# Clustered attention with a gated feed-forward: other places in the queue for the second batch's loads and rows

## The chip, the cores and the metric

The kernel runs on one core of one Trainium2 chip. The metric is the device time of one execution in microseconds (us). An engine takes its instructions in the order in which the program holds them. PE is the matmul engine (PEld its weight loads), DVE, ACT and POOL are the three elementwise engines, and SP issues nearly all transfers.

## The reference

Four batches of eight heads, 768 tokens, head width 64. Queries and keys are assigned to one of 16 centroids by the largest cosine; a query sees only keys of its own cluster. The result, 3072 tokens of 512 features, goes through a gated feed-forward.

```python
q_assign = np.argmax(np.einsum('bhsd,hcd->bhsc', q_n, c_n), axis=-1)
k_assign = np.argmax(np.einsum('bhsd,hcd->bhsc', k_n, c_n), axis=-1)
mask = q_assign[:, :, :, None] == k_assign[:, :, None, :]
scores = np.where(mask, scale * np.matmul(q, k.transpose(0, 1, 3, 2)), -1e9)
attn = softmax(scores)                      # over the keys
x = np.matmul(attn, v)                      # (tokens, 512) after regrouping the heads
out = (sigmoid(x @ w_gate) * (x @ w_val)) @ w_out
```

## The kernel before

The work goes by batch (0 to 3), and in a batch by pairs of heads (0 to 3; "first pair" is pair 0, and "second batch" is batch 1). The clock of the program is the **step**: one score matmul of 128 keys by 384 queries (L1071), its exponential on ACT (L1076) and, a few steps later, three matmuls with the values (L1094). There are 96 steps to a batch, 384 in all; a pair takes 24 of them, its two heads 12 each. Between the steps PE gets pieces of the feed-forward of the batch before (gate L537, value L553, output L870 and L999).

Before a pair's steps begin, its heads are prepared (`pair_prep`, from L1629). For each head these stages follow each other:

1. its raw keys and queries are loaded with those of the other head of the pair (`load`, L213: `kraw`, `qraw`, `vraw`, 384 KB each, three buffers to each kind);
2. `sp`: DVE casts to half precision (L1636), POOL takes the rest that the cast left (L1637); the two stand side by side in `hl`;
3. `tn`, the **turn**: SP issues a transposing transfer of `hl` into the tile `T` (L417, in the trace `T<-hl`);
4. `lg`: twelve small matmuls on PE (L441) read `T` and give the products with the centroids;
5. `pk`: DVE picks the largest and writes one-hot codes into `oh`; both heads of a pair share it;
6. `ot`: SP turns the codes (L1654, `ohT<-oh`);
7. `hp0` and `hp1`, the **rows**: SP copies the turned codes into rows 64 to 80 of the two tiles `T` (L497, two small transfers for each head). With these rows in both operands the score matmul applies the mask itself. The head's first score needs them.

The other transfers of SP are the turns of the attention's result for the feed-forward (L1125, `xTb<-xp`) and the stores (L509).

The order on every engine is set by the table `SCHED`: `at(step, f)` queues a piece of work, `run_bg` plays all pieces that are due, sorted by their step, and each engine's instructions come out in that order. A key such as `b1p3tn0` is an offset to the first step of batch 1, pair 3; `b1lk2` is one to the load of the keys of pair 2 (`lq` queries, `lv` values), added to the pair's `ld`. In batch 1 the pairs begin at steps 96, 120, 144 and 168, and batch 2 begins at 192.

```python
def go(name, off, f):
    o = SCHED.get(f"b{b}p{p}{name}", SCHED.get(f"b2{name}", off) if b > 1 else off)
    ...
    at(use + o, g)
...
at(use + o + d_, lambda b=b, p=p, side=side: load(..., SP, side, b, p))
```

The sign `E` in a key, as in `r3pl1E`, names the engine of a piece of batch 0 (A for ACT, D for DVE): here one of the two copies (L1403 on ACT, L1405 on DVE) that set the masking rows of the second half of batch 0's last pair.

Of the kernel before, what the change touches and what calls it, by code (L numbers as in the profile page):

```python
# [57 lines left out]
    "b1p2pk0": -35.5, "b1p2sp10": -50, "b1p2sp11": -47, "b1p2tn1": -42, "b1p2lg1": -28.0,  # L58
    "b1p2pk1": -27.0, "b1p2ot": -24, "b1p2hp0": -18, "b1p2hp1": -17.5, "b1p2vc": -18.0,
    "b1p2vs": -11.0, "b1p2vu": -2.5, "b1p2vt": 3, "b1p2ld": -67.5, "b1p2l20": 0, "b1p2le0":  # L60
    2.0, "b1p2l21": 0, "b1p2le1": 2.0, "b1p3sp00": -60.5, "b1p3sp01": -57, "b1p3tn0": -54,
    "b1p3lg0": -38.0, "b1p3pk0": -36.5, "b1p3sp10": -55.0, "b1p3sp11": -43.0, "b1p3tn1":
    -40.0, "b1p3lg1": -28, "b1p3pk1": -27.0, "b1p3ot": -23.5, "b1p3hp0": -13.0, "b1p3hp1":
    -12.5, "b1p3vc": -7.5, "b1p3vs": -18.5, "b1p3vu": -14.5, "b1p3vt": 4, "b1p3ld": -69.5,
# [7 lines left out]
    "dm2": 10, "dm3": 11, "dm4": 3, "la0": 3, "la1": 2, "lgop": 0, "h3ev1E": "A", "h4lo1E":  # L72
    "D", "r2hiE": "P", "r1pl0E": "A", "h5hi1E": "P", "h2hi0E": "A", "g0lo0E": "D", "h6ev1E":
    "A", "h2hi1E": "P", "h1lo1E": "D", "g1ev1E": "A", "r2ev0E": "A", "r1hiE": "P", "h4hi1E":
    "P", "r2pl1E": "A", "h3lo1E": "D", "r3pl1E": "A", "xm33": 1, "xm30": 1, "gL": 1, "rL3": 1,
    "rL2": 1, "rL1": 0, "rL0": 0, "gD": 0, "rD0": 0, "rD1": 0, "rD2": 0, "rD3": 1, "h4hi0E":
    "P", "xs00": -4, "xs10": 0, "xs01": -6, "xs11": 5.5, "xs02": 1, "xs12": 3.0, "xs03": -0.5,
    "xs13": 0, "sd": 1, "b2lk": -0.5, "b1lk0": 2.0, "b1lk1": -9, "b1lk2": -5, "b1lk3": -9.5,
    "b2lq": 0, "b1lq0": 2.5, "b1lq1": -0.5, "b1lq2": -4.9, "b1lq3": -9.4, "b2lv": 1.0, "b1lv0":
    -1, "b1lv1": 0.5, "b1lv2": 32.5, "b1lv3": 34, "ns02": 490, "ns03": 490, "ns20": 500,  # L80
    "ns21": 491, "ns22": 481, "ns23": 410, "ns30": 443, "ns31": 443, "ns32": 443, "ns33": 423,
    "h6hi1E": "P", "h1ev1E": "A", "g1hi0E": "A", "h3hi1E": "P", "g1lo0E": "D", "h1lo0E": "D",
    "r3pl0E": "A", "hM3": 0, "hM7": 1, "h1hi0E": "P", "g1hi1E": "P", "h3ev0E": "A", "g0pl0E":
# [9 lines left out]
    1, "tx": 1, "b2p3lk": 8.5, "b2p3lq": 9, "b2p3lv": 10, "b3p3lk": 8.5, "b3p3lq": 9,  # L93
    "b3p3lv": 10,
    "b3p0vs": -30, "b3p0vu": -28, "b3p0vt": -9, "b3p1lg0": -32, "b3p1pk0": -32, "fwg": [327, 327, 331, 331.5, 332, 341, 341, 344],
    "fwv": [354, 356, 357, 359, 364, 366, 370, 371], "b3p2pk1": -28.5, "b1p0sp00": -30, "b1p0sp01": -29, "b1p0sp10": -28, "b1p0sp11": -27, "b1p0tn0": -25.5, "b1p0tn1": -23.5, "b1p0lg0": -17, "b1p0pk0": -16, "b1p0lg1": -15.5, "b1p0pk1": -15.5, "b1p0ot": -14.5, "b1p0hp0": -8.5, "b1p0hp1": -8, "b2p0lk": 11, "b2p0lq": 11.5, "b2p0lv": 36, "b2p1lg1": -27, "b2p1pk1": -25.5, "nW20": 2.2, "END": 0,
}


# [1676 lines left out]
```

## Time and profile before

| | |
|---|---|
| median of 3 runs | 318.92 us (318.62 to 319.18) |
| the profiled execution | 319.96 us, of which 318.2 us span from first to last instruction |
| granted clock of PE | 1.000 |
| PE busy | 309.1 us (97%) |
| ACT, DVE, POOL busy | 241.7, 238.3, 122.0 us (76%, 75%, 38%) |
| SP's own DMA queue (q1) | 55.7% of 16 DMA engines' span, 40.75 MB |
| score matmuls | 384, 325 ns each by the modelled end |

The timeline gives for each group of instructions its start, its time, the engine, the line and the operands; a bracket at the end tells the idle time before it and what ended that. A PE row's end is modelled: the next matmul begins before it. A row of the transfers' view gives a kind of transfer, the number in the window, the size, and the time from issue to landing. SP rows show how long SP was busy with issuing.

### The profile page before, as it was taken

How to read it: one execution, taken by the hardware profiler on the slowest of the kernel's cores; microseconds unless marked ns; L12 is line 12 of the kernel's file. 1: busy time of each engine (PE TensorE's matmuls, PEld its weight loads, DVE VectorE, ACT ScalarE, POOL GpSimd, SP SyncE). 2: the span in 40 equal slices, each digit the busy share in tenths (PEclk: the TensorE clock that was granted, in tenths of full speed). 3: DMA queues.
4: the chain of work that ended last, by engine and by line, in shares of the span. 5: the costliest groups of instructions: out<-in, count | busy, mean ns of one | idle time of the engine just before them, and what ended most of it. 6: DMA issues, size and time to landing. Idle time of an engine off the chain costs nothing.

```text
span 318.2 us, 9151 instructions
## 1 busy us (share of the span) xinstructions
PE 309.1 (97%) x3444; PEld 217.0 (68%) x3444; DVE 238.3 (75%) x622; ACT 241.7 (76%) x550; POOL 122.0 (38%) x158
## 2 busy tenths in 40 slices
PE   7899999899999989999999999999999999999995
PEld 5688766555666655666777678766677678656684
DVE  6899658686887666686778688777888776678982
ACT  6788988667988877877866877788877887588621
POOL 5888447243434364423334233424212111026600
PEclk9999999999999999999999999999999999999999
DMA  7999999919699989889566467962803110300014
GB/s 212 369 262 165 269 175 170 226 34 207 185 210 248 186 196 179 230 152 198 111 186 149 135 136 104 256 175 49 111 5 82 48 27 12 146 1 1 2 35 165
DMA packets 82060, 46.24 MB, mean 145 GB/s; under 512 B 60896, under 2 KB 79584, under 8 KB 82016
## 3 DMA queue, kind: packets, MB, share of 16 engines
q1 hardware_dynamic: 77904, 40.75, 55.7%
q0 software_dynamic: 3680, 4.72, 8.9%
q8 instruction: 27, 0.44, 0.6%
q10 hardware_dynamic: 432, 0.20, 0.2%
q14 instruction: 17, 0.14, 0.2%
HBM read 28.34 MB, written 6.29 MB: 109 GB/s over the span
## 4 chain that ended last, share of the span: by engine, by line
PE 83%; DMA 9%; DVE 4%; SPq 1%; POOL 1%; issue 1%; ACT 1%; DVEq 0%
PE sc L1071 16%; PE g L537 13%; PE v L553 13%; PE av L1094 9%; PE o L999 9%; DMA T<-hl 7%; PE o L870 4%; PE lg L441 2%; PE o L704 2%; PE o_end L807 2%; PE av L704 2%; DMA kraw<-in_k_dram 2%; PE y L704 2%; PE v L633 2%; PE av L807 1%; PE o L807 1%
## 5 line engine op out<-in xcount | busy, mean ns | idle before, releaser
L1076 ACT ACTIVATE es<-sc 128x384 f16<-128x384 f32 x384 | 174.0, 492 | 42.6 <-PE sc L1071 31.3
L1071 PE MATMUL sc<-T 128*128 128x384 f16 x384 | 117.2, 325 | 0.6 <-DVE T L1405 0.2
L1094 PEld LDWEIGHTS <-es 128*128 128x128 f16 x1152 | 81.5, 98 | 35.1 <-ACT es L1076 0.2
L1094 PE MATMUL av<-va,es 128*128 128x65 f16 x1152 | 97.5, 194 | 0.0
L558 DVE SCALAR_TENSOR_TENSOR hT<-th,v 128x384 f16<-128x384 f32 x72 | 39.8, 553 | 33.3 <-PE av L1094 26.5
L377 POOL TENSOR_TENSOR xp<-t,rec 128x384 f16<-128x384 f32 (+1 forms) x30 | 21.7, 725 | 100.3 <-DVE rec L374 51.5
L553 PE MATMUL v<-xTb,wv 128*128 128x384 f16 x288 | 58.5, 326 | 0.3 <-ACT es L1076 0.2
L537 PE MATMUL g<-xTb,wg 128*128 128x384 f16 x288 | 58.5, 326 | 0.1
L543 ACT ACTIVATE th<-g 128x384 f32<-128x384 f32 x72 | 35.4, 492 | 8.4 <-PE g L537 6.1
L553 PEld LDWEIGHTS <-wv 128*128 128x128 f16 x288 | 28.0, 97 | 14.5 <-issue 0.9
L537 PEld LDWEIGHTS <-wg 128*128 128x128 f16 x288 | 28.0, 97 | 14.4 <-issue 0.3
L1071 PEld LDWEIGHTS <-T 128*128 128x128 f16 x384 | 37.0, 96 | 1.0 <-DVE T L1401 0.5
L1637 POOL TENSOR_TENSOR hl<-kraw,hl 128x384 f16<-128x384 f32 x24 | 22.2, 924 | 31.8 <-DVE hl L1636 17.5
L1637 POOL TENSOR_TENSOR hl<-qraw,hl 128x384 f16<-128x384 f32 x24 | 23.0, 958 | 12.4 <-DVE hl L1636 12.4
L372 DVE TENSOR_TENSOR t<-av,sv 128x390 f32<-128x390 f32 (+1 forms) x30 | 14.4, 480 | 7.5 <-PE av L1094 5.5
L870 PE MATMUL o<-wo,hT 128*128 128x512 f16 x72 | 19.9, 379 | 0.0
L946 DVE TENSOR_TENSOR ob<-o,ob 128x256 f32<-128x256 f32 (+1 forms) x28 | 15.0, 549 | 4.7 <-PE o L999 3.2
L713 POOL TENSOR_TENSOR hT<-T 128x384 f16<-128x384 f32 x12 | 11.8, 1004 | 16.2 <-DVE T L662 15.6
L456 DVE TENSOR_REDUCE lgs<-lg 128x192 f32<-128x384 f32 x24 | 13.2, 552 | 4.9 <-PE lg L441 4.9
L999 PE MATMUL o<-wo,hT 128*128 128x256 f16 x108 | 16.8, 272 | 0.0
L999 PEld LDWEIGHTS <-sum 128*128 128x128 f16 x144 | 14.0, 97 | 3.3
L324 POOL CAST va<-vraw 128x768 f16<-128x768 f32 x15 | 13.1, 875 | 2.3 <-DMA vraw<-in_v_dram 2.3
(207 smaller groups left out, 457.3 us busy)
## 6 DMA issues: line engine op xcount, KB each, us to landing
vraw<-in_v_dram SPq DMA_DIRECT2D x15, 384.0 KB, 5.9
kraw<-in_k_dram SPq DMA_DIRECT2D x14, 384.0 KB, 4.1
qraw<-in_q_dram SPq DMA_DIRECT2D x12, 384.0 KB, 4.5
out_dram<-ob SPq DMA_DIRECT2D x17, 256.0 KB, 2.3
wg<-in_moe_w_gate_dram POOLq DMA_DIRECT2D x2, 768.0 KB, 9.4
wv<-in_moe_w_val_dram POOLq DMA_DIRECT2D x2, 768.0 KB, 10.3
wo<-in_moe_w_out_dram POOLq DMA_DIRECT2D x2, 768.0 KB, 10.8
T<-ohT SPq DMA_DIRECT2D x48, 24.0 KB, 1.9
```

The lines of the kernel that those rows point to most:

```text
L377: (eng or POOL).tensor_tensor(x, t[:, 0:nq, 0:64], bcast(rec[:, 0:nq], 64), ALU.mult)
L537: PE.matmul(out=g[:, 0:n], lhsT=wg[fc // WQ][:, dc, fc % WQ, :], rhs=xT[:, dc, t0 : t0 + n], start=(dc == 0), stop=(dc == NDC - 1),)
L543: ACT.activation(th[:, 0:n], g[:, 0:n], AF.Tanh)
L553: PE.matmul(out=w[:, 0:n], lhsT=wv[fc // WQ][:, dc, fc % WQ, :], rhs=xT[:, dc, t0 : t0 + n], start=(dc == 0), stop=(dc == NDC - 1),)
L558: DVE.scalar_tensor_tensor(HB[b, blk][:, fc, 0:n], st[0][:, 0:n], 1.0, w[:, 0:n], ALU.add, ALU.mult)
L704: PE.matmul(out=o, lhsT=l, rhs=r, start=start and d == 0, stop=stop and d == 1, skip_group_check=True,)
L870: PE.matmul(out=o, lhsT=HB[b, blk][:, fc, bass.ts(t, 128)], rhs=wo[fc // WON][:, fc % WON, :], start=(fc == 0), stop=(fc == NFC - 1),)
L999: PE.matmul(out=st[z][:, e], lhsT=a[:, c, :], rhs=rhs[:, c, :], start=start and c + e == 0, stop=c == HF - 1, skip_group_check=True,)
L1071: PE.matmul(out=sc.rearrange("p (c t) -> p c t", t=128), lhsT=s["k"], rhs=s["q"], start=True, stop=True,)
L1076: ACT.activation(es, sc, AF.Exp, scale=SCALE)
L1094: PE.matmul(out=av[:, a0 + s["c0"] + i, :], lhsT=s["es"][:, bass.ts(i, 128)], rhs=VA[b, p][:, e, s["j"], :], start=(first and i == 0 and a ...
L1637: POOL.tensor_tensor(hl[:, :, 64:128], r, hl[:, :, 0:64], ALU.subtract)
```

## The change

Only numbers of `SCHED` change. In steps: the first pair's rows of batch 1 go from 87.5 and 88 to 86.5 and 87; the third pair's keys and queries from 71.5 to 78, its values from 109 to 90.5; the fourth pair's keys and queries from 89 to 90, its values from 132.5 to 94.5; its first head's casts from 107.5 and 111 to 106 and 108.5 and its first turn from 114 to 112. Of batch 2, the first pair's keys and queries go from 120.5 to 114 and its values from 145.5 to 109. One small copy of batch 0 goes from ACT to DVE.

```diff
-    "b1p3sp00": -60.5, "b1p3sp01": -57, "b1p3tn0": -54,
+    "b1p3sp00": -62, "b1p3sp01": -59.5, "b1p3tn0": -56,
...
-    "r3pl1E": "A"
+    "r3pl1E": "D"
...
-    "b1lk2": -5, "b1lk3": -9.5, "b1lq2": -4.9, "b1lq3": -9.4, "b1lv2": 32.5, "b1lv3": 34
+    "b1lk2": 1.5, "b1lk3": -8.5, "b1lq2": 1.6, "b1lq3": -8.4, "b1lv2": 14, "b1lv3": -4
...
-    "b1p0hp0": -8.5, "b1p0hp1": -8, "b2p0lk": 11, "b2p0lq": 11.5, "b2p0lv": 36
+    "b1p0hp0": -9.5, "b1p0hp1": -9, "b2p0lk": 4.5, "b2p0lq": 5, "b2p0lv": -0.5
```

What that makes of the order is shown at three places of SP. First, where batch 1's first two pairs are turned. `T_1467` and the next `T` (1505 before, 1501 now) are the first pair's two heads, 1572 (now 1568) and 1651 the second pair's; the raw tiles 1485 and 1497 (now 1598 and 1604) are the third pair's keys and queries. Before:

```order
L417 DMA_TRANSPOSE T_1467<-hl_1397 128x12x128
L213 DMA kraw_1485<-in_k_dram 128x2x384
L213 DMA qraw_1497<-in_q_dram 128x2x384
L417 DMA_TRANSPOSE T_1505<-hl_1431 128x12x128
L1125 DMA_TRANSPOSE xTb_312<-xp_1339 128x3x128
L417 DMA_TRANSPOSE T_1572<-hl_1478 128x12x128
L417 DMA_TRANSPOSE T_1651<-hl_1592 128x12x128
```

And now:

```order
L417 DMA_TRANSPOSE T_1467<-hl_1397 128x12x128
L417 DMA_TRANSPOSE T_1501<-hl_1431 128x12x128
L1125 DMA_TRANSPOSE xTb_312<-xp_1339 128x3x128
L417 DMA_TRANSPOSE T_1568<-hl_1478 128x12x128
L213 DMA kraw_1598<-in_k_dram 128x2x384
L213 DMA qraw_1604<-in_q_dram 128x2x384
L417 DMA_TRANSPOSE T_1651<-hl_1588 128x12x128
```

The two loads stood ahead of the first pair's second turn; now they stand ahead of the second pair's second turn.

Second, from the fourth pair's first turn (`T_2161`, now 2141) to its second (2349, now 2353). `ohT_2246` (now 2254) are the third pair's codes, the four copies from it that pair's rows, and the raw tiles 2252 and 2263 (now 2167 and 2173) are the keys and queries of batch 2's first pair. Before:

```order
L417 DMA_TRANSPOSE T_2161<-hl_2057 128x12x128
L1654 DMA_TRANSPOSE ohT_2246<-oh2_136 128x6x128
L213 DMA kraw_2252<-in_k_dram 128x2x384
L1125 DMA_TRANSPOSE xTb_1907<-xp_1945 128x6x128
L213 DMA qraw_2263<-in_q_dram 128x2x384
L497 DMA T_1858<-ohT_2246 16x768 x2
L497 DMA T_1997<-ohT_2246 16x768 x2
L417 DMA_TRANSPOSE T_2349<-hl_2151 128x12x128
```

And now:

```order
L417 DMA_TRANSPOSE T_2141<-hl_2049 128x12x128
L213 DMA kraw_2167<-in_k_dram 128x2x384
L213 DMA qraw_2173<-in_q_dram 128x2x384
L1654 DMA_TRANSPOSE ohT_2254<-oh2_136 128x6x128
L1125 DMA_TRANSPOSE xTb_1911<-xp_1949 128x6x128
L497 DMA T_1860<-ohT_2254 16x768 x2
L497 DMA T_2001<-ohT_2254 16x768 x2
L417 DMA_TRANSPOSE T_2353<-hl_2157 128x12x128
```

Here two loads that stood behind the turn of the codes now stand ahead of it.

Third, directly behind that: the loads of batch 2's second pair (2543, 2545, 2547; now 2545, 2547, 2549) and the turns of batch 2's first pair (2559 and 2683, now 2561 and 2683). Before:

```order
L213 DMA vraw_2416<-in_v_dram 128x2x384
L213 DMA kraw_2543<-in_k_dram 128x2x384
L213 DMA qraw_2545<-in_q_dram 128x2x384
L213 DMA vraw_2547<-in_v_dram 128x2x384
L417 DMA_TRANSPOSE T_2559<-hl_2446 128x12x128
L1654 DMA_TRANSPOSE ohT_2581<-oh0_134 128x6x128
L213 DMA vraw_2602<-in_v_dram 128x2x384
L1125 DMA_TRANSPOSE xTb_1907<-xp_2277 128x6x128
L417 DMA_TRANSPOSE T_2683<-hl_2552 128x12x128
```

And now:

```order
L213 DMA kraw_2545<-in_k_dram 128x2x384
L213 DMA qraw_2547<-in_q_dram 128x2x384
L213 DMA vraw_2549<-in_v_dram 128x2x384
L417 DMA_TRANSPOSE T_2561<-hl_2448 128x12x128
L1654 DMA_TRANSPOSE ohT_2583<-oh0_134 128x6x128
L1125 DMA_TRANSPOSE xTb_1911<-xp_2281 128x6x128
L417 DMA_TRANSPOSE T_2683<-hl_2554 128x12x128
```

The two value loads (2416, of the fourth pair, and 2602, of batch 2's first pair) have left this stretch. The three value loads that stood at steps 109, 132.5 and 145.5 now stand one ahead of the third pair's first turn, one ahead of the turn of the second pair's codes, and one ahead of the fourth pair's first turn, where the third pair's values stood. From the loads of batch 2's third pair on, the order of SP is the same as before.

12 rows, old and new, of the table SCHED are left out of this document.

## Prediction

> **What bounds the kernel now.** I read the page first, then the busy times by stage, then the waits, and last the timeline of the two queues that meet there. The page's busy line and three stretches of the table by stage (length, then busy time of PE, PEld, DVE, ACT, POOL):
>
> ```profile
> PE 309.1 (97%) x3444; PEld 217.0 (68%) x3444; DVE 238.3 (75%) x622; ACT 241.7 (76%) x550; POOL 122.0 (38%) x158
> 50.00:63.00 13.00, 12.15 (x135) 7.94 (x133) 10.15 (x27) 9.79 (x23) 6.54 (x8) 1.00 1.05 199
> 100.00:115.00 15.00, 14.11 (x165) 9.33 (x164) 10.66 (x32) 12.26 (x30) 6.37 (x7) 1.00 1.04 196
> 130.00:200.00 70.00, 69.93 (x782) 50.20 (x780) 53.15 (x137) 53.04 (x119) 22.72 (x27) 1.00 0.71 160
> ```
>
> PE sets the time. From 130 us on it has no hole to speak of (69.93 of 70), so a microsecond gained or lost ahead of that reaches the end almost whole. Its holes are in the stretches that the change touches: 0.85 us in the first, 0.89 us in the second. The waits tell what they are for:
>
> ```profile
> PEld L441 <- DMA T<-hl: 2.6, 4, 1.0
> PE lg L441 <- DMA T<-hl: 1.9, 3, 0.9
> ```
>
> The logits (L441) stand in PE's queue and wait for a turn `T<-hl` to land; everything behind them waits too. PE's timeline gives the four places (start, modelled time, line, and in the bracket the idle time):
>
> ```profile
> 57.99 0.32 PE L1071 MATMUL sc<-T 128*128 128x384 f16 x1
> 58.16 0.81 PE L537 MATMUL g<-xTb,wg 128*128 128x384 f16 x4
> ...
> 58.89 0.33 PE L1071 MATMUL sc<-T 128*128 128x384 f16 x1
> 59.79 0.47 PE L441 MATMUL lg<-cm,T 128*128 128x32 f16 x12 [0.57 <-DMA T<-hl]
> ...
> 98.23 0.26 PE L1094 MATMUL av<-va,es 128*128 128x65 f16 x3
> 98.59 0.46 PE L441 MATMUL lg<-cm,T 128*128 128x32 f16 x12
> ...
> 111.99 0.26 PE L1094 MATMUL av<-va,es 128*128 128x65 f16 x3
> 113.14 0.47 PE L441 MATMUL lg<-cm,T 128*128 128x32 f16 x12 [0.89 <-DMA T<-hl]
> ...
> 120.85 0.26 PE L1094 MATMUL av<-va,es 128*128 128x65 f16 x3
> 121.52 0.47 PE L441 MATMUL lg<-cm,T 128*128 128x32 f16 x12 [0.41 <-DMA T<-hl]
> ```
>
> The first two rows show an undisturbed pair: the score lasts 0.32 but the next matmul starts 0.17 after it, so each hole is its bracket plus 0.17. That makes 0.74 us at 59.8 (first pair of batch 1, second head), 1.06 at 113.1 and 0.58 at 121.5 (batch 2: first pair's second head, second pair's first). At 98.6 (fourth pair's second head) the start is 0.36 behind the last one, 0.10 over its 0.26, so 0.27 with the overlap. Sum 2.65 us. One more hole follows the first as its echo: ACT is behind and PE waits for it.
>
> ```profile
> 62.74 0.48 ACT L1403 ACTIVATE T<-oh_ps 16x384 f16<-16x384 f16 x1
> 62.77 0.81 PE L553 MATMUL v<-xTb,wv 128*128 128x384 f16 x4 [0.19 <-ACT es L1076]
> ```
>
> By the same count this one hole is 0.36 us. The copy on ACT is the one that the change gives to DVE.
>
> **Place one: the turn at 59.8.** SP's queue, the three transfers of it (time from issue to landing, last column), and the POOL row that completes that turn's data:
>
> ```profile
> 51.73 0.91 POOL L1637 TENSOR_TENSOR hl<-qraw,hl 128x384 f16<-128x384 f32 x1 [0.30 <-DVE hl L1636]
> ...
> 52.74 0.58 SPq L213 DMA_DIRECT2D kraw<-in_k_dram  x1
> 53.36 0.47 SPq L213 DMA_DIRECT2D qraw<-in_q_dram  x1
> 53.94 1.94 SPq L417 DMA_TRANSPOSE T<-hl  x1
> ...
> kraw<-in_k_dram SPq DMA_DIRECT2D x1, 384.0 KB, 4.3
> qraw<-in_q_dram SPq DMA_DIRECT2D x1, 384.0 KB, 4.9
> T<-hl SPq DMA_TRANSPOSE x1, 5.8
> ```
>
> Landings: keys 52.74 + 4.3 = 57.0, queries 58.3, turn 59.7. They land in the order of issue, about 1.3 us apart for a load and 1.5 for the turn: the queue behaves as one line. The data was ready at 52.64, so with the loads gone the turn is issued at 52.74, 1.2 us sooner, and has 2 x 1.3 us less ahead of it. Even if only the sooner issue counts it lands at 59.7 - 1.2 = 58.5; PE asks at 58.89 + 0.17 = 59.06. So the hole goes on either reading: **+0.74 us**. Of the echo I take +0.4: 0.36 by its row, and the copy's 0.48 us leaves ACT; DVE takes at most 0.5 us more there (it is busy 10.15 of 13). The bounds are 0 and 0.8.
>
> A rule that speaks against this: the Trainium skill, page "DMA: Bandwidth & Descriptors", section "Queues, rings and completion order", says that completion is not in order of issue for one issuing engine, so a load ahead need not hold the turn back. The three landings here are in order, so the trace does not show it at this place; what it would give is the second rival.
>
> The loads now stand ahead of the second pair's second turn, which has room:
>
> ```profile
> 58.27 3.00 SPq L417 DMA_TRANSPOSE T<-hl  x2
> ...
> 67.44 0.46 PE L441 MATMUL lg<-cm,T 128*128 128x32 f16 x12
> ```
>
> It is asked for 6 us after SP has issued it; two loads cost 2.6. Price 0.
>
> **Place two: the third pair's first turn.** The first pair's rows go ahead of an `xTb` turn. I assume that SP has room for their 2.49 us there, so that the loads and the turn behind move up by as much. In exchange one value load joins them.
>
> ```profile
> 69.23 2.49 SPq L497 DMA_DIRECT2D T<-ohT  x4
> ...
> 72.97 2.13 SPq L417 DMA_TRANSPOSE T<-hl  x1
> ...
> T<-hl SPq DMA_TRANSPOSE x1, 6.1
> ...
> 79.95 0.20 PE L441 MATMUL lg<-cm,T 128*128 128x32 f16 x2
> ```
>
> Today it lands at 79.0 and PE asks at 79.95. Up by 2.49, back by 1.3 for the extra load: 77.9. PE, ahead by 0.74 + 0.4, asks at 78.8. Room 0.9; I take 0. Without the credit it lands at 80.3 and PE waits 1.5; but then PE comes as much later to place three and waits so much less there, so the sum hardly moves. Behind it the turn of the second pair's codes also gets a value load ahead (1.3 us against the 2.49).
>
> **Place three: the fourth pair's second turn, at 98.6.** This is where the change can pay for itself twice.
>
> ```profile
> 84.65 0.96 POOL L1637 TENSOR_TENSOR hl<-qraw,hl 128x384 f16<-128x384 f32 x1 [0.76 <-DVE hl L1636]
> ...
> 85.64 1.33 SPq L417 DMA_TRANSPOSE T<-hl  x1
> 87.19 2.02 SPq L1654 DMA_TRANSPOSE ohT<-oh  x1
> ...
> 92.78 2.45 SPq L497 DMA_DIRECT2D T<-ohT  x4
> 95.28 1.35 SPq L417 DMA_TRANSPOSE T<-hl  x1
> ```
>
> SP cannot issue the rows (92.78) before the turned codes have landed, and the second turn stands behind them. So the chain is: codes land (92.7), rows 2.5 us, turn 3.3 us from issue to landing (95.28 to just before 98.59). Whatever delays the codes delays PE 5.8 us later. Now two loads stand ahead of the codes: +2.6 us. Against that, the first turn no longer waits for POOL at 85.61 (its casts stand 1.5 and 2.5 steps sooner, at about 0.65 us a step), so the chain starts about 1.0 us sooner; and a pause in this stretch should cost it less. The transfers between 89.5 and 91.5 hold one instruction fetch:
>
> ```profile
> q8 instruction: 1, 0.02, 3.6%
> ```
>
> I take it to come with PE's progress (PE has 3444 matmuls and as many weight loads, far the most instructions), so about 1.1 us sooner; today turn and codes are in flight then and both stand still, afterwards the loads are in flight and can go on beside it. I take 1.2 us for that (bounds 0 and 1.5; an estimate from the first turn's landing, some 1.5 us later than place one's spacing). The codes then land at 92.7 + 2.6 - 1.0 - 1.2 = 93.1, the second turn at 98.9. PE, 0.74 + 0.4 + 0.27 ahead, would ask at 98.59 - 1.4 = 97.2 and waits 1.7 us. It passes this place at 98.9 against 98.59 today: all that was gained by then is gone, and 0.3 us more. The bounds for the landing: 97.2 (no wait) and 101.1 (2.6 in full, no credit).
>
> **Place four: batch 2's first turns.** Two value loads leave this stretch.
>
> ```profile
> 105.45 0.58 SPq L213 DMA_DIRECT2D vraw<-in_v_dram  x1
> ...
> 107.44 2.17 SPq L417 DMA_TRANSPOSE T<-hl  x1
> ...
> 114.56 3.90 SPq L417 DMA_TRANSPOSE T<-hl  x1
> ```
>
> The turn issued at 107.44 lands as PE starts at 113.14. Without the load at 105.45 it is issued at least 0.6 us sooner with one load (1.3) less ahead: 1.9 against a hole of 1.06, which goes: **+1.06**. What follows on SP (rows, three loads, the turn at 114.56) moves up by as much, so the loads ahead of that turn have drained more when it comes; its hole of 0.58 goes, **+0.58** (bounds 0 and 0.58, since its own data may hold it). Nothing comes in their place: from there on the order is the old one and PE has the room.
>
> **The sum.** 98.59 - 98.9 + 1.06 + 0.58 = 1.3 us; less 0.1 for small waits, **1.2 us** gained. In general the gain is 100.2 minus the landing at place three, at most 3.0 us. Against the profiled execution (318.2 us span, 319.96 with what lies around it) that makes 318.8; the median of the runs is 318.92, 0.3% below that execution, so I forecast 318.92 - 1.2 = **317.7 us**. About 0.2% (0.64 us) is what a measurement of this kernel can tell from no change.
>
> **The rivals.**
> 1. *The codes behind the loads become the bound (slower).* If the landing at place three comes after 100.2, it costs more than place four returns. The full 2.6 us without credit gives 101.1, so 0.9 us lost: 319.8. With slower loads (up to 0.4 us more) 320.2. For it: SP's strict order and the 5.8 us chain. Against it: the sooner casts. Chance 0.28.
> 2. *The loads hold nothing back, or gain and loss cancel.* If turns are not in line behind loads, place four keeps 1.06 + 0.58, the turn at place three lands at 98.5 as today, and PE waits there for what it gained at place one: 318.9, no change. The same time comes from a landing near 100.2. Chance 0.17.
> 3. *Everything is hidden.* The codes come early enough for a landing by 97.2 and the whole 3.0 us stay: 315.9. It needs all credits and one load overlapped. Chance 0.10.
>
> The forecast, a landing between 97.5 and 99.5, has 0.45, and its own range is 316.2 to 318.2.
>
> **How the numbers follow.** Faster by over 0.2% are the forecast and rival 3: 0.55. Within 0.2%: 0.17. Slower: 0.28. The range reaches from 316.0, nearly rival 3, to 320.2, the dear end of rival 1.
>
> **What would show it.** In the changed profile the wait of L441 for `T<-hl` should be gone at the first pair (near 59), near 111 and near 119, and one wait of 1 to 2.5 us should stand at the fourth pair's second head, with the rows (L497) on SP just ahead of the turn. No hole there would mean rival 3; holes left near 111 and 119 would mean that loads do not hold turns; a hole over 3 us there, or a new one at 79 to 84, means slower.

## The result: 1.1% slower, and the profile after

| | before | after |
|---|---|---|
| median | 318.92 us (318.31 to 319.18, 5 runs) | 321.67 us (321.16 to 323.73, 5 runs) |
| ratio, 95% interval | | 1.0109 (1.0068 to 1.0149) |
| the profiled execution | 319.96 us, span 318.2 | 321.67 us, span 319.9 |
| granted clock of PE | 1.000 | 0.999 |

The change costs 2.75 us where 1.2 us of gain were forecast. The clock does not explain it: the three runs of the kernel after at a granted clock of 0.998 or more took 321.16 to 321.67 us (the two at 0.993 and 0.994 took 323.4 and 323.7). The waits of the kernel after, that of the logits (L441) for a turn (us in total, times, longest):

```profile
PE lg L441 <- DMA T<-hl: 4.4, 2, 2.3
```

Three waits of 1.9 us in all have become two of 4.4. The stretches of the table by stage, with 70 to 100 added (length, then busy time of PE, PEld, DVE, ACT, POOL):

```profile
70.00:100.00 30.00, 27.31 (x312) 17.64 (x310) 21.07 (x53) 23.29 (x55) 11.57 (x13) 1.00 0.80 191
100.00:115.00 15.00, 13.04 (x155) 8.90 (x156) 9.27 (x28) 11.28 (x28) 4.74 (x6) 1.00 0.97 189
130.00:200.00 70.00, 69.93 (x768) 49.74 (x765) 53.00 (x136) 53.79 (x121) 23.76 (x29) 1.00 0.69 158
```

The same stretch 70 to 100 before:

```profile
70.00:100.00 30.00, 29.88 (x344) 19.37 (x343) 22.11 (x57) 25.09 (x60) 13.13 (x14) 1.00 0.90 193
```

From 130 us on nothing has changed (69.93 us busy in both; from 200 us to the end PE is idle for 3.4 us in both). PE lost its time between 70 and 115, at two turns. Its timeline after, at place one, place two and place three:

```profile
58.50 0.33 PE L1071 MATMUL sc<-T 128*128 128x384 f16 x1
58.66 0.46 PE L441 MATMUL lg<-cm,T 128*128 128x32 f16 x12
...
61.63 0.81 PE L553 MATMUL v<-xTb,wv 128*128 128x384 f16 x4 [0.19 <-ACT es L1076]
...
80.80 0.47 PE L441 MATMUL lg<-cm,T 128*128 128x32 f16 x12 [2.03 <-DMA T<-hl]
...
101.96 0.41 PE L441 MATMUL lg<-cm,T 128*128 128x32 f16 x10 [2.33 <-DMA T<-hl]
```

The hole at place one is gone; the small wait for ACT at 61.6 that was taken for its echo is still there. New is the wait at the third pair's first turn, and the one at the fourth pair's second turn is 2.33 us. SP after, around place two, with the times from issue to landing of the two that matter:

```profile
58.28 0.57 SPq L213 DMA_DIRECT2D kraw<-in_k_dram  x1
...
59.50 1.97 SPq L417 DMA_TRANSPOSE T<-hl  x1
61.57 2.03 SPq L1654 DMA_TRANSPOSE ohT<-oh  x1
67.41 2.50 SPq L497 DMA_DIRECT2D T<-ohT  x4
70.01 1.21 SPq L1125 DMA_TRANSPOSE xTb<-xp  x1
...
72.39 0.47 SPq L213 DMA_DIRECT2D vraw<-in_v_dram  x1
72.98 2.15 SPq L417 DMA_TRANSPOSE T<-hl  x1
```

```profile
ohT<-oh SPq DMA_TRANSPOSE x1, 5.8
T<-hl SPq DMA_TRANSPOSE x1, 7.8
```

And the same piece before:

```profile
61.96 1.21 SPq L1654 DMA_TRANSPOSE ohT<-oh  x1
67.95 1.18 SPq L1125 DMA_TRANSPOSE xTb<-xp  x1
```

```profile
ohT<-oh SPq DMA_TRANSPOSE x1, 2.8
```

Before, the codes landed at 61.96 + 2.8 = 64.8, and SP stood idle until the `xTb` turn could go at 67.95. The rows (2.5 us) would have fitted there. After, the two loads (58.28, and the queries at 58.89) stand ahead of the second pair's second turn and of these codes, which land at 61.57 + 5.8 = 67.4. The rows need them, so SP waits for them, `xTb` goes at 70.01, and the third pair's first turn is issued at 72.98, as before (72.97). It now has one more load ahead and lands at 80.8.

Around place three, after, from the turn of the second pair's codes on:

```profile
76.83 1.44 SPq L1654 DMA_TRANSPOSE ohT<-oh  x1
...
82.87 2.85 SPq L497 DMA_DIRECT2D T<-ohT  x4
...
86.92 1.60 SPq L417 DMA_TRANSPOSE T<-hl  x1
88.57 0.57 SPq L213 DMA_DIRECT2D kraw<-in_k_dram  x1
89.19 0.51 SPq L213 DMA_DIRECT2D qraw<-in_q_dram  x1
89.80 1.22 SPq L1654 DMA_TRANSPOSE ohT<-oh  x1
...
96.13 2.44 SPq L497 DMA_DIRECT2D T<-ohT  x4
98.67 1.43 SPq L417 DMA_TRANSPOSE T<-hl  x1
```

```profile
T<-hl SPq DMA_TRANSPOSE x1, 6.4
kraw<-in_k_dram SPq DMA_DIRECT2D x1, 384.0 KB, 5.5
qraw<-in_q_dram SPq DMA_DIRECT2D x1, 384.0 KB, 6.0
ohT<-oh SPq DMA_TRANSPOSE x1, 6.3
T<-hl SPq DMA_TRANSPOSE x1, 3.2
```

The landings are 93.3, 94.1, 95.2, 96.1, in the order of issue, and the last turn at 101.9. Before, the codes landed at 92.7, and the rows that stand ahead of the first turn went at 81.19:

```profile
81.19 2.43 SPq L497 DMA_DIRECT2D T<-ohT  x4
```

### The profile page after: what moved, and what is told of

Read it like the earlier page. It is cut to its first block, busy times and chain, and to the rows that moved or that the text cites. A ratio compares the mean times of both kernels' runs of the same rounds, so it can differ in the third digit from the quotient of the medians.

```text
span 319.9 us, 9156 instructions
## 1 busy us (share of the span) xinstructions
PE 307.9 (96%) x3444; PEld 216.6 (68%) x3444; DVE 239.0 (75%) x623; ACT 240.8 (75%) x549; POOL 121.9 (38%) x158
## 4 chain that ended last, share of the span: by engine, by line
PE 87%; DVE 5%; DMA 3%; ACT 1%; issue 1%; POOL 0%; ACTq 0%; DVEq 0%; POOLq 0%
PE sc L1071 17%; PE v L553 14%; PE g L537 14%; PE av L1094 10%; PE o L999 9%; PE o L870 4%; DMA T<-hl 3%; PE lg L441 2%; PE o L704 2%; PE o_end L807 2%; PE av L704 2%; PE v L633 2%; PE y L704 2%; PE av L807 1%; PE o L807 1%; PE z L704 1%
## 5 line engine op out<-in xcount | busy, mean ns | idle before, releaser
L441 PE MATMUL lg<-cm,T 128*128 128x32 f16 x300 | 11.5, 176 | 4.4 <-DMA T<-hl 4.4
```

## The experiments

Three theories stood at the start. A: each wait comes from what stands ahead of a turn, or of its codes, in SP's one line. B: the value loads alone do it. C: a lower clock. To them came D, after the first look at further executions: place one's hole belonged to one execution. The granted clock was 0.992 to 1.0 in all runs. C falls for the change (see above) and for the runs that show the loss at a full clock; it bears on the size of e10 and a little on e5, and that is said there. All medians, each against runs of the kernel before on the same chip, and PE's idle time between 70 and 130 us in the profiled execution (60 less PE's busy time in that stretch of the table by stage):

| kernel | median us | before | ratio, 95% interval | PE idle, us |
|---|---|---|---|---|
| before: first profile, two more | | | | 1.42; 1.20, 0.65 |
| after | 321.67 | 318.92 | 1.0109 (1.0068 to 1.0149) | 4.64 |
| e1: after, keys and queries behind the codes | 319.78 | 318.76 | 1.0033 (1.0019 to 1.0048) | 1.97 |
| e2: after, value loads back | 321.43 | 318.76 | 1.0092 (1.0065 to 1.0119) | 3.00 |
| e4: after, both back | 319.71 | 318.76 | 1.0032 (1.0014 to 1.0050) | 2.58 |
| e5: e1, third pair's values behind its turn | 320.74 | 318.71 | 1.0056 (1.0033 to 1.0079) | 3.20 |
| e3: before, place one's loads moved | 318.77 | 318.76 | 0.9996 (0.9979 to 1.0013) | 1.05 |
| e8: e3, rows a step sooner | 319.21 | 319.09 | 0.9990 (0.9967 to 1.0014) | 1.56 |
| e9: e3, fourth pair's casts and first turn sooner, copy on DVE | 319.29 | 319.09 | 1.0017 (0.9996 to 1.0038) | 2.29 |
| e10: before, place three's loads moved | 320.99 | 319.09 | 1.0062 (1.0043 to 1.0081) | 3.03 |
| e6: before, value loads in an idle slot | 317.80 | 318.71 | 0.9967 (0.9949 to 0.9985) | 0.02 |
| e7: e6, a turn ahead of the rows | 318.16 | 319.09 | 0.9976 (0.9954 to 0.9999) | 0.05 |

The idle time is that of one execution. For e4, e9 and e10 that one lay 1.0, 1.6 and 0.9 us over the median (320.70, 320.87 and 321.85 us), so their last column is likely too high for a typical run.

### Undoing parts of the change: e1, e2, e4

e1 puts keys and queries of batch 2's first pair back behind the codes, e2 the three value loads where they were, e4 both.

```diff
 e1:  - "b2p0lk": 4.5, "b2p0lq": 5
      + "b2p0lk": 11, "b2p0lq": 11.5
 e2:  - "b1lv2": 14, "b1lv3": -4, "b2p0lv": -0.5
      + "b1lv2": 32.5, "b1lv3": 34, "b2p0lv": 36
```

> The changed kernel with one part undone: keys and queries of batch 2's first pair stand behind the turn of the third pair's codes again (steps 120.5 and 121). Theory A (each wait of PE comes from loads that stand ahead of that turn or of its codes in SP's one line): the wait at the fourth pair's second head falls from 2.5 us to 0.3 to 0.8, the 2.0 us at the third pair's first head stay, and the time falls by 1.5 to 2.1 against the changed kernel, to about 319.8. Theory B (the three value loads alone do the harm): no change, 321.7. Theory C (the loss is a lower granted clock): no change in the waits' sum against the time, and 321 to 323 with a clock under 1.

e1 took 319.78 us, 1.9 us less than after. PE's timeline of e1 at place two and place three:

```profile
81.06 0.47 PE L441 MATMUL lg<-cm,T 128*128 128x32 f16 x12 [1.37 <-DMA T<-hl]
...
100.20 0.47 PE L441 MATMUL lg<-cm,T 128*128 128x32 f16 x12 [0.32 <-DMA T<-hl]
```

The wait at place three falls from 2.33 to 0.32 us. These two loads are the largest part of the loss.

> The changed kernel with the three value loads back at steps 109, 132.5 and 145.5. Theory A: the wait at the third pair's first head falls from 2.0 us to under 0.5; the one at the fourth pair's second head stays over 1.5, since keys and queries still stand ahead of the codes; holes of about 1 us come back at batch 2's first turns; time 320 to 321. Theory B: the time falls to 318.9 or below. Theory C: no change.

e2 took 321.43 us, hardly less than after and a little over A's 320 to 321. Its wait at place two is gone, but the one at place three (2.4 us) is as long as ever and one at batch 2's first pair is back: what PE no longer loses at one turn it loses at the next. B falls.

> The changed kernel with both undone: value loads back, and keys and queries of batch 2's first pair behind the codes. What is left are place one, the rows a step sooner, the fourth pair's sooner casts and the copy on DVE. Theory A: no wait over 0.5 at the third pair's first head, one of 0.3 to 1.0 at the fourth pair's second, the old holes at batch 2's first turns; 318.3 to 319.2. Theory C: above 320.

e4 took 319.71 us, like e1, so the value loads cost and save about the same: with them place two waits and batch 2 does not, without them the other way round. A's own time, 318.3 to 319.2, was missed by 0.5 us; e8 and e9 look for that.

### Place one alone, and the kernel before again: e3, b1, b2

```diff
 e3:  - "b1lk2": -5, "b1lq2": -4.9
      + "b1lk2": 1.5, "b1lq2": 1.6
```

> The kernel before with one part done alone: the third pair's keys and queries at steps 78 and 78.1, behind the first pair's second turn. Theory A: the wait of 0.6 at 59.8 and its echo go (1.1 us), the turn at the fourth pair's second head lands as before and PE waits there for most of what it gained, so 318.5 to 319.0. A theory by which every hole on PE is worth its length gives 317.8.

e3 took 318.77 us against 318.76: the move that was to give 0.74 us and an echo gives nothing. A had expected as much, with the gain given back at place three, and D says the same, so e3 alone does not tell the two apart. So the kernel before was profiled twice more.

> The kernel before itself, for a second profile, since the one that the prediction was read from was an execution 1.2 us over the median. Theory D (the hole at 59.8 belonged to that one execution: its first turn of batch 1 landed 6.0 us after issue, 3.2 in four other kernels): the first turn lands 3.2 to 3.9 us after issue, the hole at place one is under 0.2 us, the span is about 317.0. Rival (the hole is the kernel's own): turn 5.5 to 6.5 us, hole 0.5 to 0.9, and the gain at place one was given back further on.

> The same once more, as the question is how often that hole is there. Theory D: as before, hole under 0.2 us at place one; the holes at the fourth pair's second head (0.2 to 0.5) and at batch 2's first pair (0.8 to 1.1) are there each time.

The first turn of batch 1, from issue to landing, in the first profile of the kernel before, and then in the second, with PE at place one in the second:

```profile
T<-hl SPq DMA_TRANSPOSE x1, 6.0
```

```profile
T<-hl SPq DMA_TRANSPOSE x1, 3.2
```

```profile
59.17 0.33 PE L1071 MATMUL sc<-T 128*128 128x384 f16 x1
59.33 0.45 PE L441 MATMUL lg<-cm,T 128*128 128x32 f16 x12
```

In the second the logits start 0.16 us behind the score, an undisturbed pair; in the third profile 0.20. The waits of the third show what is left of the four places, one wait at batch 2's first pair:

```profile
PE lg L441 <- DMA T<-hl: 0.6, 1, 0.6
```

The first turn took 6.0 us in the first profile alone and 3.2 us in the third, too. Three further kernels, e6, e7 and e10, leave place one as it was; there, too, the first turn took 3.2 us and the logits start 0.16 to 0.30 us behind the score. D holds: of six profiles with this order, the hole stands in one, the execution of 319.96 us, which was 1.04 us over the median.

### Place two's wait moved on: e5

```diff
 e5:  e1, and   - "b1lv2": 14
                + "b1lv2": 15
```

> The changed kernel with keys and queries of batch 2's first pair behind the codes (as in the first experiment), and the third pair's values behind that pair's first turn (step 91.5) in place of ahead of it. Theory A: the turn lands 1.3 to 2.9 us sooner and the wait of 1.5 us at the third pair's first head falls to under 0.4; the codes behind it land as before, so the wait at the fourth pair's second head grows by what PE gained, to 1.0 to 2.0, and the time falls by 0 to 0.5 against that experiment, to about 319.5. By a theory in which each hole counts in full it falls by 1.5, to 318.3.

The third pair's values now go behind its first turn. The wait at place two is gone, as A says, but the time rose from 319.78 to 320.74 us, where A expected 319.5 (the eight of its eleven runs at a granted clock of 0.998 or more have a median of 320.6). PE at place three of e5:

```profile
100.94 0.46 PE L441 MATMUL lg<-cm,T 128*128 128x32 f16 x12 [1.75 <-DMA T<-hl]
```

The load now stands ahead of the second pair's codes, and their rows ahead of the fourth pair: the delay was moved down SP's line, not taken out of it.

### Place three alone: e10

```diff
 e10: - "b2p0lk": 11, "b2p0lq": 11.5        (in the kernel before)
      + "b2p0lk": 4.5, "b2p0lq": 5
```

> The kernel before with one edit: keys and queries of batch 2's first pair go ahead of the turn of the third pair's codes. Theory A (SP's one line): the codes land 2.6 to 3.4 us later (95.3 to 96.1), the rows behind them and the fourth pair's second turn as much (it lands 101.2 to 102), PE waits 2.5 to 3.2 us there, and gets back about 1.0 at batch 2's first pair: 320.2 to 321.0. Theory of the prediction (credit for the sooner start and the pause, which this kernel only partly has): the turn lands by 100.5, time 319.5 or less. Theory B (values alone): 318.7.

e10 took 320.99 us, 0.62% or 2.0 us more than before (1.4 to 2.6): this one edit alone. Its SP and PE at place three:

```profile
87.31 0.84 SPq L213 DMA_DIRECT2D kraw<-in_k_dram  x1
...
88.80 1.22 SPq L1654 DMA_TRANSPOSE ohT<-oh  x1
...
94.39 2.45 SPq L497 DMA_DIRECT2D T<-ohT  x4
96.92 1.30 SPq L417 DMA_TRANSPOSE T<-hl  x1
```

```profile
100.21 0.47 PE L441 MATMUL lg<-cm,T 128*128 128x32 f16 x12 [1.43 <-DMA T<-hl]
...
115.62 0.46 PE L441 MATMUL lg<-cm,T 128*128 128x32 f16 x12 [1.29 <-DMA T<-hl]
```

The chain codes, rows, turn is the predicted one, and the edit costs time. Neither theory has all of it right. The time is what A expected. But the codes landed at 94.3 and the turn at 100.2, a microsecond sooner than A's 95.3 to 96.1 and 101.2 to 102, and within the 100.5 of the prediction's theory; 1.43 us are lost at place three (2.5 to 3.2 expected), and batch 2's first pair, at 115.6, gives nothing back. Part of the 2.0 us may be the clock: six of the eleven runs have a granted clock of 0.992 to 0.995, the profiled one among them, whose clock stood at 0.50 from 11.5 to 14.9 us, far ahead of the edit. The five runs at 0.998 or more have a median of 320.48 us, so the edit itself costs between 1.4 and 2.0 us.

### The rest: e8 and e9

e4 holds neither value loads nor place three's loads and is still 0.3% over before, while e3 is not. Between them stand the rows, and the fourth pair's casts and first turn, which go sooner (its loads go a step later), with the copy on DVE.

```diff
 e8:  e3, and   + "b1p0hp0": -9.5, "b1p0hp1": -9
 e9:  e3, and   + "b1lk3": -8.5, "b1lq3": -8.4, "b1p3sp00": -62, "b1p3sp01": -59.5,
                + "b1p3tn0": -56, "r3pl1E": "D"
```

> The kernel before with the moved loads of place one and, besides, the first pair's rows a step sooner; nothing else of the change. Open so far is why the change without its value loads and with keys and queries behind the codes still takes 319.7, 0.9 us more than place one's loads alone (318.8). Theory rows: SP waits for the landing of the first pair's codes (near 67.4, or 65 where no load is late) ahead of the third pair's xTb turn and its loads, which go 1 to 2 us later; the time is 319.3 to 319.7 with a hole at the third pair's turns or behind. Rival (the rest: the fourth pair's sooner casts and turn and the copy given to DVE): this run stays at 318.8 and PE's step 144 within 0.3 us of place one's loads alone.

> The kernel before with the moved loads of place one and the rest of the change apart from rows, values and batch 2's keys and queries: the fourth pair's loads one step later, its casts and first turn 1.5 to 2.5 steps sooner, and the copy of one plane given to DVE. Theory rows expects no cost here: 318.8 (318.5 to 319.1). Its rival expects the whole 0.9 us here: 319.5 to 319.9, with the hole at the fourth pair's second head or the waits for DVE and ACT grown by as much.

The rows alone cost nothing that can be measured. e9 lies at 1.0017 (0.9996 to 1.0038), between both expectations; its profiled execution has 2.29 us of idle PE against e3's 1.05, but that execution took 320.87 us, 1.6 over e9's median, so the difference proves little. Rows and casts together were not run. Where the 0.3% sits stays open.

### Another place for the values: e6 and e7

If SP's line is the limit, the value loads belong where the line is empty: in the kernel before, between the first pair's codes and the `xTb` turn. In e6 one load goes there, the third pair's; the other two take steps 109 and 132.5, at which a value load stood before. So the load that has left its place is the one at step 145.5, which stood on SP at 105.45, ahead of a turn of batch 2's first pair.

```diff
 e6:  - "b1lv2": 32.5, "b1lv3": 34, "b2p0lv": 36        (in the kernel before)
      + "b1lv2": 6.5, "b1lv3": 10.5, "b2p0lv": 23
 e7:  e6, and   - "b1p3tn1": -40.0
                + "b1p3tn1": -42.2
```

> The kernel before with its three value loads each one slot sooner: the third pair's behind the turn of the first pair's codes (step 83, where SP waits for data), the fourth pair's where the third's stood (109), batch 2's first where the fourth's stood (132.5). Nothing gets a load ahead of it that had none, and the turn at place four loses one. Theory A: the hole of 0.8 to 1.1 at batch 2's first pair, second head, falls under 0.3, all else stays: 317.6 to 318.2. If it stays at 318.7 the hole does not come from that load.

e6 took 317.80 us, 0.33% less than before (0.15% to 0.51%), and beats both kernels. Its SP around the slot, and its stretch 100 to 115:

```profile
61.60 1.21 SPq L1654 DMA_TRANSPOSE ohT<-oh  x1
62.86 0.57 SPq L213 DMA_DIRECT2D vraw<-in_v_dram  x1
67.28 1.19 SPq L1125 DMA_TRANSPOSE xTb<-xp  x1
```

```profile
100.00:115.00 15.00, 15.00 (x179) 9.91 (x177) 10.85 (x30) 13.06 (x31) 7.11 (x8) 1.00 0.87 216
```

The load goes behind the codes and costs nothing; `xTb` goes at 67.28. PE is busy 15.00 of 15 where it was 14.11: the hole of batch 2's first pair comes from the value load ahead of its second turn, as the prediction had it.

> The kernel before with the three value loads in SP's idle slot (as in the run before it that gave 317.80), and the fourth pair's second turn put ahead of the third pair's rows, so that it no longer stands behind the chain codes, rows, turn. Theory A (every wait of PE here comes from what stands ahead of a turn in SP's one line): the turn is issued some 2.5 us sooner, lands by 95.5, and the hole of 0.1 to 0.4 us at the fourth pair's second head goes; the rows are issued 1.3 us later and the third pair's values, which need them, have room. Time 317.5 (317.2 to 317.8). Rival (the turn stands ahead of the rows only by waiting longer for its own data, so the rows come late): a new hole behind the rows of 0.5 us or more, time 318.3 or over.

e7 did no better, 318.16 us, which is neither A's 317.2 to 317.8 nor the rival's 318.3 or over. Its SP, and the landing times of the two rows shown:

```profile
91.18 0.57 SPq L213 DMA_DIRECT2D qraw<-in_q_dram  x1
91.85 1.41 SPq L417 DMA_TRANSPOSE T<-hl  x1
```

```profile
qraw<-in_q_dram SPq DMA_DIRECT2D x1, 384.0 KB, 5.1
T<-hl SPq DMA_TRANSPOSE x1, 6.1
```

The turn is issued 2.5 us sooner than in e6 (94.39) and lands at 98.0, not sooner (e6: 97.7), for the query load ahead lands at 96.3 only. Here an earlier issue behind a load in flight was worth nothing; the expectation of 95.5 was wrong.

## Why the prediction was wrong

The step that failed is the landing at place three, 98.9 in the prediction and 101.9 in the run. Its two credits, 1.0 us for a sooner start and 1.2 us for the pause, did not come, and the start was 1.3 us later instead: the second pair's codes had a value load ahead, their rows came later (82.87 instead of 81.19), and the first turn stands behind these; the credit of 2.49 us at place two that was to outweigh this was assumed and not there. The sign that the prediction had named for a loss, a new hole at 79 to 84, stood at 80.8.

**Place one** was a hole of the profiled execution. The sum went by differences to a run that was 1.04 us over the median, and they were then taken off the median (318.92 - 1.2). The +0.74 cannot be had from the typical run, which has no such hole. It is not what made the forecast wrong, for in the sum it counts only through the time at which PE asks at place three, and PE waits there. The echo (+0.4) was not one: the wait at 61.6 stayed with the hole gone. The loads moved there had "room" only as far as the turn behind them goes; that the first pair's codes come next in line was not followed.

**Place two** failed at the assumed credit of 2.49 us. The slot existed before (64.8 to 67.95), but the change's own first edit closed it by putting two loads ahead of the codes that the rows need. The text did work out the case without the credit (landing 80.3, wait 1.5), and it came, a little larger: 80.8, wait 2.03. It also said that the sum would hardly move, since PE would wait as much less at place three. That fails because place three came later as well.

**Place three** had the right chain and the wrong landing: 101.9 instead of 98.9. By terms, for the codes (92.7 before, 93.1 predicted, 96.1 measured): the two loads cost about 2.1 instead of 2.6 (the codes land 2.8 us behind the first turn, before 0.7); the sooner start, taken as -1.0, was +1.3, since SP came to the first turn at 86.92 instead of 85.64: ahead of it stand the second pair's rows, and their codes had a value load ahead too; and of the 1.2 us for the pause nothing arrived at the codes. In e10 the two loads cost 1.9 us by the same count. The sooner casts were worth little by themselves, too: in e9, which has them without the value loads, the first turn was issued at 85.18 and landed at 92.2, in e3 without them at 84.92 and 91.5.

The pause itself changed as supposed. The instruction fetch was to come about 1.1 us sooner with PE; it began at 89.7 before and at 91.1 after, for PE was later. The stretch behind it, before and then after (the last number is GB/s moved):

```profile
90.50:91.50 1.00, 1.00 (x12) 0.61 (x9) 1.00 (x5) 1.00 (x3) 0.54 (x1) 1.00 0.06 6
91.20:92.20 1.00, 1.00 (x13) 0.68 (x12) 1.00 (x3) 0.84 (x4) 0.41 (x2) 1.00 0.93 259
```

Before, with the first turn and the codes ahead in the line, the transfers all but stood still; after, with the two loads between them, they went on. Yet the first turn took 6.4 us to land both times (85.64 to 92.05 before), and the codes came 2.8 us behind it. Why the transfers that went on in the pause did not bring the codes sooner is not shown.

**Place four** was right: both holes went once the value loads had left (no wait of L441 after 102 in the kernel after, nor in e1 and e6). In the kernel after, PE also comes there later, which alone could hide a hole; e6, where PE is not late and the hole is gone, rules that out. Its size, 1.64 us, was that execution's too; its brackets were 0.89 and 0.41 us, and the two other profiles of before have one hole each there, of 0.9 and of 0.6.

**The rule of the sum** held: the gain is 100.2 minus the landing, 100.2 - 101.9 = -1.7, and the two profiled executions stand at 319.96 and 321.67. The other 1.0 us of the measured 2.75 is the first execution's distance from its median. So rival 1 named the mechanism, with its threshold; its full price of 101.1 was still 0.8 short, because it held the delay of the loads to be the only one. Rival 2 falls: in the kernel after and in e7 the landings keep the order of issue, and in none of the fourteen profiles did a transfer of SP land ahead of one that SP had issued before it. The Trainium skill, page "DMA: Bandwidth & Descriptors", section "Queues, rings and completion order", says that completion is not in order of issue for one issuing engine; at the places looked at here it was.

## What to carry to other kernels

Edits to one queue are not added up one by one: play the whole new order through, each transfer with what it needs and what stands ahead, since one edit may fill the idle slot that another counts on. Move a load into a stretch in which the queue waits for something else, not ahead of the first link of a chain that ends at the bounding engine. And look at a second profile of the kernel before, above all when the first lies over the median, before a hole in it is counted as a gain.

## What was not expected of the hardware

- The same turn, with nothing changed ahead of it, took 6.0 us in one execution of the kernel before and 3.2 us in two others and in e6, e7 and e10. Why is open.
- A turn issued 2.5 us sooner landed no sooner (98.0 against 97.7) behind a load that was in flight and landed at 96.3: the load's landing, not the time of issue, set it.
- Of 34 executions of the kernel before on one chip, 32 spread from 316.8 to 320.5 us, so that effects of 0.2% to 0.3% needed a dozen runs on each side.
- Behind one instruction fetch the transfers moved 6 GB/s for a microsecond where a turn and the codes stood ahead in the line, and 259 GB/s where two loads stood between these.
